# Attention and two expert layers in one kernel: recomputed key blocks, shared PSUM banks, and a move of weight preparation

## The chip, the cores and the metric

The kernel runs on 1 core of a Trainium2 chip. The metric is the device time of the whole program in microseconds (us), as the median of several runs. The profile is one execution recorded by the hardware profiler.

## The reference

Three layers follow each other. N = 8 x 3072 = 24576 tokens, D = 256, 8 experts, hidden width F = 1024.

```python
# attention, 8 batches, S = 3072, z has 64 columns
scores = z @ z.T / S                    # the same z on both sides
x = u * (np.maximum(scores, 0) ** 2 @ v)
# first expert layer: all 8 experts on all tokens
P = exp(x @ w_gate - max)               # then 8 rounds of row and column normalisation
y = sum_e P[:, e] * (np.maximum(x @ w1[e], 0) @ w2[e])
# second expert layer: one expert per token (argmax of a cosine), scaled by its gate
out = gate * (np.maximum(y @ w1b[e], 0) @ w2b[e])
```

## The kernel before

All matrices are split into two float16 halves (high and low), and a product is the sum of high x high, high x low and low x high, so a logical product costs three matmuls. The three layers run one after the other on TensorE (PE).

**Attention (the first 2265 us).** There are 8 batches; in each, 6 chunks `qc` of 512 queries, and in each chunk 24 key blocks `kt` of 128 keys: 1152 steps. The scores are symmetric. A *direct* block computes its scores (`emit_S`, two matmuls of 512 columns), ScalarE (ACT) applies ReLU and squares to `hl`, an engine squares once more in float32 (`sq`), and VectorE (DVE) forms the low half (`emit_low`). In chunk `qc` the direct blocks are those with `kt // 4 >= qc`. Blocks with `kt // 4 > qc` are also stored to DRAM (`store`, 256 KB each), and a later chunk, whose *old* blocks `kt // 4 < qc` are the mirror of these, reads them back with a DMA transpose, two key blocks at a time (`load_turned`, 512 KB, into five buffers named `turned` and `ext`). `chunk_order` spreads the old blocks evenly among the 24 steps. `emit_AV` multiplies a block with `v16`: for each of four query tiles one matmul of 512 columns and one of 256 into its own PSUM bank `o0` to `o3`. Scores run 5 steps ahead of `emit_AV` (`LEAD`).

At a chunk's end the four banks are copied to `osb` (two by ACT, two by DVE), and `chunk_end` lets GpSimd (POOL) add the two halves and multiply by `u`. It then makes a float16 split, transposes it by DMA and stores it for the next layer.

**Background.** Side work is cut into generators that `Background` advances by one piece per step: lane `end` (chunk ends), `prep` (the next batch's z and v), `w` (expert weights) and `x` (tiles for the next layer). A lane with rate r moves once in r steps. Lane `w` loads each expert's weights twice (maximum, then split), writes the split weights to DRAM, first for the first expert layer (m = 0, rate 1.0) and then for the second (m = 1, rate 1.45), and must be done before the last chunk but one. The SP queue issues all these DMAs in the order in which the program is written, and each transfer is cut into packets that 16 DMA engines move.

**First expert layer (about 2265 to 9790 us).** 768 units, each a quarter of an expert on 1024 tokens: 21 matmuls of 512 columns (line 856) and 48 of 256 columns (line 938), with sums on DVE, ACT and POOL. `tick` moves the lanes four times per unit. The 12 superblocks have 64 units each. `tile_end` finishes each 512 tokens: it picks the expert, and writes a row with the token's split values, its expert's scale `iab` and gate.

**Second expert layer (from about 9790 us).** 67 jobs of 512 or 256 tokens of one expert, `job_first` (line 1377) and `job_second` (lines 924, 925), then `evac2`, which scales the result by a number from the row.

Of the kernel before, what the change touches and what calls it, by code (L numbers as in the profile page):

```python
# [4 lines left out]
F32 = mybir.dt.float32  # L5
# [6 lines left out]
P = 128  # L12
D = 256
# [73 lines left out]
def program(tc, u, v, z, wg, w1a, w2a, emb, tau, w1b, w2b, out, pool, psum, dram):  # L87
# [14 lines left out]
    wd = [dram.tile([E, P, W1N + 8 * 512], F16, name="wd0"), dram.tile([E, P, 2, 8 * 512], F16, name="wd1")]  # L102
    rows_d = dram.tile([E * R + PART, ROW], F16, name="rows_d")

    def small(name, n=1, dt=F32):
# [31 lines left out]
    def all_max(dst, src, n, waits=4):  # L137

        d = dram.tile([P, n], F32, name="amax_d")
        SP.dma_start(out=d, in_=src)  # L140
        for _ in range(waits):
            yield
        rows = small(("junk0", "prod5")[n - 1], n * P)
# [73 lines left out]
    raw = []  # L217
    loads = []

    def next_raw():  # L220

        while loads and len(raw) < 3:
            raw.append(loads.pop(0)())
        return raw.pop(0)
# [9 lines left out]
    def weight_scales(m, e):  # L234
# [25 lines left out]
        )  # L260
        yield

    def pair_split(t, e, c, o, s):
# [236 lines left out]

    def chunk_end(b, qc, osb, ut):
        T0 = (b * QC + qc) * 4
        w = m4([P, 4, D], F32, "w")
        for t in range(4):
            o = osb[t // 2][:, t % 2]
            POOL.tensor_tensor(out=w[:, t, :], in0=o[:, 0:D], in1=o[:, D:2 * D], op=ALU.add)
            yield
        for t in range(4):
            POOL.tensor_tensor(out=w[:, t, :], in0=w[:, t, :], in1=ut[:, t, :], op=ALU.mult)
            yield  # L510
# [57 lines left out]
    bg.lane("prep", 2)  # L568
    bg.lane("w", 1.0)
    bg.lane("x")  # L570
# [69 lines left out]
    with tc.manual_schedule():  # L640
# [8 lines left out]
        for _ in gg:  # L649
            pass  # L650
        def slower():
            bg.lane_rate("w", 1.45)
            return
            yield

        for m in range(2):
            if m:
                bg.add("w", slower())
            for e in range(E):
                plan_loads(m, e)  # L660
                bg.add("w", weight_scales(m, e))
                bg.add("w", weight_split(m, e))

        def chunk_order(qc):
            own, old = list(range(4 * qc, KT)), list(range(4 * qc))
            early = [(2 * j + 3) * len(old) // (2 * KT) > (2 * j + 1) * len(old) // (2 * KT) for j in range(KT)]

            j = LEAD - 1  # L670
            if early[j]:
                k = early.index(False, j)
                early[j], early[k] = False, True
            res = [(old if e else own).pop(0) for e in early]
            assert sorted(res) == list(range(KT))
            return res
# [3 lines left out]
        for b, qc, kt in steps:  # L680
            if kt // 4 >= qc:
# [37 lines left out]
        def emit_S(b, qc, kt):  # L719
# [33 lines left out]
        def store():  # L753
            hl, b, qc, kt = stores.pop(0)
            k = kt % 4 * P
            SP.dma_start(out=stored[b % 2, qc, kt // 4][k:k + P], in_=hl)

        def emit_AV(b, qc, kt, first, last):
            if kt // 4 >= qc:
# [12 lines left out]

        gens = {}

        def attn_pre(i):
            b, qc, kt = steps[i]
            if i % KT == 0 and qc == 0 and b > 0:
                bg.finish("prep", gens[b])
            direct = kt // 4 >= qc
            if direct:  # L780
                emit_S(b, qc, kt)
            if stores:
                store()
            if len(late) > direct:
                emit_low()

        def attn_main(i):
# [33 lines left out]
def moe(tc, st):  # L821
# [220 lines left out]
    def tile_end(i, x2):  # L1042
# [86 lines left out]
        yield  # L1129
        DVE.tensor_tensor(out=key, in0=oh, in1=iab[1][:, None, :].to_broadcast([P, 4, E]), op=ALU.mult)  # L1130
        DVE.tensor_reduce(out=km, in_=key, op=ALU.add, axis=AX.X)
        yield
        row32 = row.rearrange("p t c -> p (t c)").bitcast(F32).rearrange("p (t c) -> p t c", t=4)
        DVE.scalar_tensor_tensor(out=km, in0=ab, scalar=0.25, in1=km, op0=ALU.mult, op1=ALU.mult)
        DVE.tensor_tensor(out=row32[:, :, 256], in0=km, in1=gt, op=ALU.mult)
        yield
# [182 lines left out]
    def load_job_weights(j):  # L1319
# [8 lines left out]
        SP.dma_start(out=w2t, in_=src[bass.ds(re, 1), :, 1, :].rearrange("o p (f d) -> p (o f) d", f=8))  # L1328
        tab["w", j] = (w1t, w2t)

# [11 lines left out]
    def evac2(j):  # L1342
        ids = tab.pop(("x", j))[1]
        nt = job_size(j) // P
        y = m4([P, nt, D], F32, "yo")
        for t in range(nt):
            c = ids[:, t, 0:1].bitcast(F32)
            s = pool.tile([P, TOK], F32, name="r", tag="r", bufs=3)
# [160 lines left out]
```

## Time and profile before

| what | value |
|---|---|
| median of 3 runs | 10973.49 us (10967.61 to 10974.76) |
| the profiled execution, its own time | 10976.46 us |
| its span | 10974.8 us |
| PE busy over the span | 10573.4 us (96%) |
| DVE, ACT, POOL busy | 6904.8, 4380.1, 3981.6 us |

The shares of the whole span mix three layers with different limits, so each layer has to be read by itself. The DMA share is the mean busy share of the 16 DMA engines. [...]

### The profile page before, as it was taken

What the parts mean: (1) busy time and instruction counts of PE and PEld (TensorE: products, weight loads), DVE (VectorE), ACT (ScalarE), POOL (GpSimd) and SP (SyncE); (2) the same over time, 40 slices, a digit from 0 to 9 for tenths busy, and PEclk for the clock granted to TensorE, in tenths of its full rate; (3) what the DMA queues carried; (4) which work ended last, traced back from release to release, by engine and by line L of the source; (5) the groups of instructions that cost most, each with busy time, mean ns of one, the idle gap of its engine ahead of it and who ended that gap; (6) DMA issues with size and microseconds to landing.
All of it is one profiled execution on the core that took longest, in us unless ns stands there. A gap on an engine that the chain in (4) does not pass through costs nothing. (4 is left out here: it accounts for less than half of the span.)

```text
span 10974.8 us, 181329 instructions
## 1 busy us (share of the span) xinstructions
PE 10573.4 (96%) x72192; PEld 6934.6 (63%) x72192; DVE 6904.8 (63%) x11785; ACT 4380.1 (40%) x7819; POOL 3981.6 (36%) x3649
## 2 busy tenths in 40 slices
PE   7888888899999999999999999999999999999999
PEld 3444444466666666666666666666666666665456
DVE  6777766667666666666665666666666666654333
ACT  4444444433443434444443444444443444333233
POOL 4555555633232233323223333323223332223333
PEclk9999999999999999999999999999999999999999
DMA  7999999831111111111111111111111111125556
GB/s 199 235 235 235 234 236 230 223 91 40 49 50 46 47 46 47 52 42 57 40 55 41 53 42 52 47 42 57 45 48 46 50 49 46 46 80 161 152 168 194
DMA packets 1214292, 1071.97 MB, mean 98 GB/s; under 512 B 931008, under 2 KB 1048256, under 8 KB 1183872
## 3 DMA queue, kind: packets, MB, share of 16 engines
q1 hardware_dynamic: 1194336, 1007.77, 33.4%
q0 software_dynamic: 19104, 52.59, 1.4%
q8 instruction: 565, 9.26, 0.4%
q14 instruction: 287, 2.35, 0.1%
HBM read 592.28 MB, written 245.82 MB: 76 GB/s over the span
## 5 line engine op out<-in xcount | busy, mean ns | idle before, releaser
L938 PE MATMUL o<-w2t,hl 128*128 128x256 f16 x36864 | 4279.2, 273 | 0.0
L938 PEld LDWEIGHTS <-hl 128*128 128x128 f16 x36864 | 3609.2, 98 | 747.5 <-issue 1.1
L856 PE MATMUL r<-xs,w1t 128*128 128x512 f16 x16128 | 3753.8, 379 | 21.5 <-DVE blocks L912 10.9
L911 POOL TENSOR_TENSOR blocks<-prod,terms 128x512 f32<-128x512 f32 x768 | 1339.9, 1745 | 4942.5 <-ACT hl L903 4925.4
L856 PEld LDWEIGHTS <-w1t 128*128 128x128 f16 x16128 | 1568.1, 98 | 1583.5 <-issue 31.4
L892 DVE SCALAR_TENSOR_TENSOR hl<-r,hl 128x512 f16<-128x512 f32 x768 | 531.1, 692 | 1375.3 <-ACT hl L899 1373.9
L899 ACT ACTIVATE hl<-r 128x512 f16<-128x512 f32 x768 | 458.6, 597 | 2055.1 <-PE r L856 2055.1
L892 DVE SCALAR_TENSOR_TENSOR hl<-blocks,hl 128x1024 f16<-128x1024 f32 x768 | 960.5, 1251 | 305.3 <-ACT hl L917 273.2
L885 DVE TENSOR_TENSOR terms<-r,terms 128x512 f32<-128x512 f32 x768 | 530.3, 690 | 817.5 <-ACT prod L881 658.2
L879 ACT ACTIVATE terms<-r 128x512 f32<-128x512 f32 x768 | 458.5, 597 | 1239.6 <-PE r L856 849.8
L903 ACT ACTIVATE hl<-terms 128x512 f16<-128x512 f32 x768 | 484.1, 630 | 1058.6 <-DVE terms L902 1058.6
L917 ACT ACTIVATE hl<-blocks 128x1024 f16<-128x1024 f32 x768 | 807.1, 1051 | 0.0
L770 PE MATMUL o<-v,hl 128*128 128x512 f16 x1792 | 640.1, 393 | 84.3 <-ACT osb L801 50.4
L730 ACT ACTIVATE r<-h 128x512 f32<-128x512 f32 x672 | 397.5, 592 | 798.9 <-PE h L725 739.7
L1383 DVE SCALAR_TENSOR_TENSOR hl<-h,hl 128x512 f16<-128x512 f32 (+1 forms) x536 | 304.1, 568 | 654.2 <-ACT hl L1382 632.9
L1377 PE MATMUL h<-xt,w1t 128*128 128x512 f16 (+1 forms) x3216 | 628.2, 332 | 6.6 <-DVE hl L1383 3.2
L735 POOL TENSOR_TENSOR zt<-r 128x512 f32<-128x512 f32 x336 | 387.3, 1154 | 681.4 <-ACT r L730 625.5
L924 PE MATMUL o<-w2t,hl 128*128 128x512 f16 x1648 | 569.7, 381 | 21.8 <-DVE r L1350 21.0
L770 PE MATMUL o<-v,turned 128*128 128x512 f16 x1536 | 534.0, 389 | 56.0 <-DMA turned<-at 39.6
L892 DVE SCALAR_TENSOR_TENSOR hl<-terms,hl 128x512 f16<-128x512 f32 x768 | 531.9, 693 | 75.9
L1382 ACT ACTIVATE hl<-h 128x512 f16<-128x512 f32 (+1 forms) x536 | 267.3, 499 | 772.6 <-PE h L1377 750.5
L771 PE MATMUL o<-v,hl 128*128 128x256 f16 x1792 | 504.4, 282 | 61.3 <-DVE hl L745 61.1
(240 smaller groups left out, 12613.3 us busy)
## 6 DMA issues: line engine op xcount, KB each, us to landing
w1t<-wd SPq DMA_DIRECT2D x192, 896.0 KB
w2t<-wd SPq DMA_DIRECT2D x163, 1024.0 KB
at<-hl SPq DMA_DIRECT2D x288, 256.0 KB
w1t<-wd SPq DMA_DIRECT2D x67, 1024.0 KB
wraw<-in_moe_w SPq DMA_DIRECT2D x112, 512.0 KB
at<-ext SPq DMA_DIRECT2D x192, 256.0 KB
ut<-in_u SPq DMA_DIRECT2D x48, 512.0 KB
xT_d<-xt SPq DMA_DIRECT2D x48, 512.0 KB
```

Of the source, the lines that this page charges most:

```text
L770: PE.matmul(o, lhsT=tiles[t][0], rhs=vt, start=first, stop=False)
L771: PE.matmul(o[:, D:2 * D], lhsT=tiles[t][1], rhs=vt[:, 0:D], start=False, stop=last)
L856: PE.matmul(r, lhsT=w[:, p % 2, blk, a, :], rhs=x[:, b, :], start=start and j == 0, stop=j == 2, skip_group_check=True,)
L885: DVE.tensor_tensor(out=u2, in0=r[1], in1=c1, op=ALU.add)
L892: eng.scalar_tensor_tensor(out=dst, in0=src, scalar=0.0, in1=hi, op0=ALU.max, op1=ALU.subtract)
L899: ACT.activation(out=f0[:, 0, h0], in_=r[0], func=AF.Relu)
L903: ACT.activation(out=f0[:, 0, h1], in_=c12, func=AF.Relu)
L911: POOL.tensor_tensor(out=terms[1][:, 1], in0=terms[2], in1=u3, op=ALU.add)
L917: ACT.activation(out=f1[:, 0], in_=c2, func=AF.Relu)
L924: PE.matmul(o_ps[t], lhsT=hl[:, 0, t * P:(t + 1) * P], rhs=w2t[:, f, :], start=f == 0, stop=False)
L938: PE.matmul(o, lhsT=hl[:, a, t * P:(t + 1) * P], rhs=w2t[:, f, b * D:(b + 1) * D], start=f == 0 and t % 2 == 0 and a + b == 0, stop=f == 7 ...
L1377: PE.matmul(h, lhsT=w1t[:, a, c, f * P:(f + 1) * P], rhs=xt[:, 2 * b + c, :], start=i == 0, stop=i == 5)
```

## The change

Six edits, all visible in the diff:

1. `direct(qc, kt)` is now `kt // 2 >= 2 * qc - 1`: each chunk from the second on computes two key blocks more itself and reads one pair of blocks less. The half of a stored block that nobody reads any more is not stored.
2. `emit_AV` uses three matmuls of 256 columns for a query tile, and two query tiles share a PSUM bank. Two banks make a set, and chunks alternate between two sets. The copies to `osb` and POOL's additions are gone; `chunk_end` multiplies by `u` straight from PSUM on DVE.
3. The odd extra squares are all on ACT; before, every second of them was on DVE.
4. Lane `w` runs at rate 1.9 through attention and prepares only m = 0. The weights with m = 1 are planned at the start of the second superblock of the first expert layer, at rate 6, with two raw buffers instead of three.
5. Because these weights come later, `tile_end` no longer multiplies by `iab`. It is written to DRAM (`iab_d`), each job loads it (`iabj`), and `evac2` multiplies it in with a small DVE operation.
6. The broadcast row of the weights' maximum uses a buffer of the common pool `m4`.

```diff
-    bg.lane("w", 1.0)
+    bg.lane("w", 1.9)
...
+        def direct(qc, kt):
+            return kt // 2 >= 2 * qc - 1
 
         def chunk_order(qc):
-            own, old = list(range(4 * qc, KT)), list(range(4 * qc))
+            own, old = ([kt for kt in range(KT) if direct(qc, kt) == d] for d in (True, False))
...
             if n % 2 == 0:
                 POOL.tensor_tensor(out=a, in0=r, in1=r, op=ALU.mult)
-            elif n % 4 == 1:
+            else:
                 ACT.activation(out=a, in_=r, func=AF.Square)
-            else:
-                DVE.tensor_tensor(out=a, in0=r, in1=r, op=ALU.mult)
...
-            SP.dma_start(out=stored[b % 2, qc, kt // 4][k:k + P], in_=hl)
+            n = 1 if kt // 4 == qc + 1 else 2
+            SP.dma_start(out=stored[b % 2, qc, kt // 4][k:k + P, 0:n], in_=hl[:, 0:n])
...
-                if first:
-                    acc_ps[t] = psum.tile([P, 2 * D], F32, name=f"o{t}", tag=f"o{t}", bufs=1)
-                o = acc_ps[t]
-                PE.matmul(o, lhsT=tiles[t][0], rhs=vt, start=first, stop=False)
-                PE.matmul(o[:, D:2 * D], lhsT=tiles[t][1], rhs=vt[:, 0:D], start=False, stop=last)
+                if first and t % 2 == 0:
+                    n = (b * QC + qc) % 2 * 2 + t // 2
+                    acc_ps[t // 2] = psum.tile([P, 2 * D], F32, name=f"o{n}", tag=f"o{n}", bufs=1)
+                o = acc_ps[t // 2][:, t % 2 * D:(t % 2 + 1) * D]
+                for a, h in ((0, 0), (0, 1), (1, 0)):
+                    PE.matmul(
+                        o, lhsT=tiles[t][a], rhs=vt[:, h * D:(h + 1) * D], start=first and t % 2 == 0 and a + h == 0,
+                        stop=last and a == 1, skip_group_check=True,
+                    )
...
-                osb = [m4([P, 2, 2 * D], F32, "osb") for _ in range(2)]
-                for t in range(4):
-                    if t % 2:
-                        DVE.tensor_copy(out=osb[t // 2][:, t % 2], in_=acc_ps[t])
-                    else:
-                        ACT.activation(out=osb[t // 2][:, t % 2], in_=acc_ps[t], func=AF.Copy)
                 bg.finish("end")
-                bg.add("end", chunk_end(b, qc, osb, ut.pop((b, qc))))
+                bg.add("end", chunk_end(b, qc, dict(acc_ps), ut.pop((b, qc))))
...
-        for t in range(4):
-            o = osb[t // 2][:, t % 2]
-            POOL.tensor_tensor(out=w[:, t, :], in0=o[:, 0:D], in1=o[:, D:2 * D], op=ALU.add)
-            yield
-        for t in range(4):
-            POOL.tensor_tensor(out=w[:, t, :], in0=w[:, t, :], in1=ut[:, t, :], op=ALU.mult)
+        yield
+        for j in range(2):
+            DVE.tensor_tensor(
+                out=w[:, 2 * j:2 * j + 2, :], in0=acc[j].rearrange("p (t d) -> p t d", t=2),
+                in1=ut[:, 2 * j:2 * j + 2, :], op=ALU.mult,
+            )
             yield
...
+        if (i, e, p) == (SB, 0, 0):
+            g["depth"][0] = 2
+            bg.lane_rate("w", 6)
+            g["plan_weights"](1)
         if i >= NTILE - SB and e == E - 1 and p % 2:
+            bg.finish("w")
...
+        cs = tmp("wb", 4)[:, 0:nt]
+        DVE.tensor_scalar(out=cs, in0=ids[:, :, 0].bitcast(F32), scalar1=tab["w", j][2], scalar2=None, op0=ALU.mult)
```

The first place is the SP queue in the first batch, third chunk (`qc` = 2). Rows with `at` on the left store a block for a later chunk (`at_2_3`: from chunk 2 for chunk 3), `turned` and `ext` are pairs read back, `vring` and `zr` the next batch's v, `wraw` and `wpair` weights, `xt` a chunk end. Before:

```order
L756 DMA at_2_3_226<-hl_67 128x1024
L708 DMA_TRANSPOSE turned<-at_0_3_219 128x4x512
L756 DMA at_2_3_226<-hl_67 128x1024
L285 DMA wd_64<-wpair 128x1792
L756 DMA at_2_3_226<-hl_68 128x1024
L207 DMA wraw<-in_moe_w 128x4x256
L756 DMA at_2_3_226<-hl_68 128x1024
```

And in the changed kernel:

```order
L758 DMA at_2_3_227<-ext 128x512 x2
L758 DMA at_2_3_227<-hl_68 128x512
L392 DMA zt<-zt 64x1024 x4
L407 DMA vring<-in_v 128x2x256 x4
L543 DMA_TRANSPOSE xt<-xr 128x4x128 x4
L758 DMA at_2_3_227<-hl_68 128x512
```

The four stores for the next chunk have half their width, and the weights' DMAs stand further apart.

The second place is DVE at a chunk's end in a middle batch, where `o` is an accumulator bank, `hl` and `ext` are low halves of blocks, and `wraw` is weight work. Before:

```order
L271 TENSOR_TENSOR wraw<-wraw 128x128
L799 COPY osb<-o_4466 128x512
L799 COPY osb<-o_4472 128x512
L494 SCALAR_TENSOR_TENSOR v_4702<-zr,fk,v_4702 128x256 x2
L745 TENSOR_TENSOR hl_67<-zt,hl_67 128x2x256
```

And in the changed kernel:

```order
L746 TENSOR_TENSOR hl_69<-zt,hl_69 128x2x256
L510 TENSOR_TENSOR w<-o_7171,ut 128x512
L271 TENSOR_TENSOR wraw<-wraw 128x128
L272 TENSOR_TENSOR wraw<-wraw 128x128
L746 TENSOR_TENSOR ext<-zt,ext 128x2x256
L510 TENSOR_TENSOR w<-o_7178,ut 128x512
```

The two copies that stood together at the chunk's end became two products, one step apart and behind low halves of the next chunk.

The third place is DVE in the first expert layer, in one and the same unit (`terms`, `blocks` and `hl` are the unit's own sums, `acc` an expert's end). Before:

```order
L912 TENSOR_TENSOR blocks<-r_33133,terms 128x512
L1220 SCALAR_TENSOR_TENSOR acc<-o_32884,L,acc 128x256 x2
L1220 SCALAR_TENSOR_TENSOR acc<-o_32898,L,acc 128x256 x2
L885 TENSOR_TENSOR terms<-r_33223,terms 128x512
L892 SCALAR_TENSOR_TENSOR hl_21440<-blocks,hl_21440 128x1024
```

And in the changed kernel:

```order
L915 TENSOR_TENSOR blocks<-r_37038,terms 128x512
L1219 SCALAR_TENSOR_TENSOR acc<-o_36783,L,acc 128x256 x2
L1219 SCALAR_TENSOR_TENSOR acc<-o_36797,L,acc 128x256 x2
L319 SCALAR_TENSOR_TENSOR wout<-wraw,sc_79,wout 128x256
L888 TENSOR_TENSOR terms<-r_37128,terms 128x512
L895 SCALAR_TENSOR_TENSOR hl_25298<-blocks,hl_25298 128x1024
```

One weight operation stands ahead of the unit's own sums.

## Rows read from the trace of the kernel before

**Rows 1.** The page's span in 40 equal slices: DMA share in tenths.

```profile
DMA  7999999831111111111111111111111111125556
```

**Rows 2.** Busy time by stretch: attention, batches 3 and 8, and inner stretches.

```profile
core 0: us, PE busy (x) PEld busy (x) DVE busy (x) ACT busy (x) POOL busy (x), PEclk, DMA share, GB/s
41.00:2265.00 2224.00, 1925.70 (x11313) 1071.09 (x11312) 1533.73 (x2734) 958.21 (x1689) 1252.86 (x1405) 0.95 0.93 230
...
625.00:907.00 282.00, 241.55 (x1417) 133.30 (x1416) 202.78 (x376) 118.91 (x207) 156.60 (x176) 0.96 0.95 239
...
2008.00:2265.00 257.00, 237.36 (x1418) 133.85 (x1417) 158.82 (x255) 123.30 (x232) 159.53 (x174) 0.95 0.83 225
...
500.00:2000.00 1500.00, 1297.87 (x7630) 721.73 (x7631) 1036.84 (x1871) 620.06 (x1083) 848.61 (x960) 0.95 0.97 233
3000.00:9000.00 6000.00, 5995.89 (x43180) 4145.25 (x43179) 3885.85 (x6433) 2449.26 (x4351) 1863.88 (x1416) 1.00 0.15 48
```

**Rows 3.** DMA view from 500 to 2000 us: packets by size, and two kinds of issues.

```profile
DMA packets 611371, 349.50 MB, mean 233 GB/s; under 512 B 470379, under 2 KB 550325, under 8 KB 611253
...
turned<-at SPq DMA_TRANSPOSE x136
...
ext<-at SPq DMA_TRANSPOSE x34
```

**Rows 4.** DMA view from 3000 to 9000 us.

```profile
DMA packets 130469, 289.56 MB, mean 48 GB/s; under 512 B 90576, under 2 KB 90576, under 8 KB 120144
```

**Rows 5.** Groups by line, 41 to 2265 us: busy us, mean ns, idle before and releasers.

```profile
L770 PE MATMUL o<-v,hl 128*128 128x512 f16 x1792 | 640.1, 393 | 84.3 <-ACT osb L801 50.4 <-DVE osb L799 25.9 <-ACT hl L732 7.9
L770 PE MATMUL o<-v,turned 128*128 128x512 f16 x1536 | 534.0, 389 | 56.0 <-DMA turned<-at 39.6 <-DVE osb L799 15.5 <-ACT osb L801 0.6
...
L735 POOL TENSOR_TENSOR zt<-r 128x512 f32<-128x512 f32 x335 | 386.0, 1154 | 681.2 <-ACT r L730 625.3 <-DVE hl L745 28.7 <-DVE ext L745 10.9
L745 DVE TENSOR_TENSOR hl<-zt,hl 128x512 f16<-128x512 f32 x448 | 378.9, 852 | 200.6 <-POOL zt L735 104.5 <-ACT zt L737 53.6 <-ACT hl L732 40.7
...
L732 ACT ACTIVATE hl<-r 128x512 f16<-128x512 f32 x445 | 280.2, 630 | 208.2 <-DMA at<-hl 188.9 <-DVE hl L745 3.3 <-DVE zb L354 3.3
...
L509 POOL TENSOR_TENSOR w<-w,ut 128x256 f32<-128x256 f32 x188 | 160.5, 870 | 0.0
...
L312 POOL TENSOR_SCALAR wout<-wraw,sc 128x256 f16<-128x256 f32 x192 | 156.2, 819 | 26.4 <-DVE sc L132 14.4 <-DMA zr<-in_v 8.9 <-issue 2.8
...
L243 DVE TENSOR_REDUCE wmx<-wraw 128x1 f32<-128x256 f32 x256 | 101.3, 408 | 40.6 <-DMA wraw<-in_moe_w 40.6
```

**Rows 6.** Timeline from 5000 us: start, duration, engine, instructions.

```profile
5001.67 2.78 PE L938 MATMUL o<-w2t,hl 128*128 128x256 f16 x24
5002.27 1.23 DVE L892 SCALAR_TENSOR_TENSOR hl<-blocks,hl 128x1024 f16<-128x1024 f32 x1 [0.28 <-ACT hl L917]
5004.29 2.10 PE L856 MATMUL r<-xs,w1t 128*128 128x512 f16 x9
...
5006.23 2.78 PE L938 MATMUL o<-w2t,hl 128*128 128x256 f16 x24
```

**Rows 7.** Timeline from 10441 us, the end of a job.

```profile
10442.38 1.26 ACT L1352 ACTIVATE r<-o,ids 128x512 f32<-128x512 f32 x2
...
10442.51 0.69 DVE L1383 SCALAR_TENSOR_TENSOR hl<-h,hl 128x512 f16<-128x512 f32 x1 [1.90 <-ACT hl L1382]
...
10443.12 1.53 DVE L1350 TENSOR_SCALAR r<-o,ids 128x512 f32<-128x512 f32 x2
...
10444.28 0.38 PE L924 MATMUL o<-w2t,hl 128*128 128x512 f16 x1
```

**Rows 8.** Groups by line, 9800 to 10975 us.

```profile
L924 PE MATMUL o<-w2t,hl 128*128 128x512 f16 x1648 | 569.7, 381 | 21.8 <-DVE r L1350 21.0 <-DVE acc L1220 0.6
...
L1063 DVE SCALAR_TENSOR_TENSOR row<-acc,xci,row 128x256 f16<-128x256 f32 x16 | 8.8, 554 | 0.0
```

**Rows 9.** Groups by line, 2800 to 9790 us.

```profile
L1063 DVE SCALAR_TENSOR_TENSOR row<-acc,xci,row 128x256 f16<-128x256 f32 x176 | 143.7, 836 | 0.0
```

More of the change, by code (lines that the diff above doesn't have):

```diff
@@ L103, in program @@
     rows_d = dram.tile([E * R + PART, ROW], F16, name="rows_d")
+    iab_d = dram.tile([E, P], F32, name="iab_d")
     def small(name, n=1, dt=F32):
@@ L142, in all_max @@
             yield
-        rows = small(("junk0", "prod5")[n - 1], n * P)
+        rows = small("junk0", P) if n == 1 else m4([P, n * P], F32, "rows")
         SP.dma_start(out=rows, in_=d.rearrange("p n -> (p n)").partition_broadcast(P))
@@ L218, in program @@
     loads = []
+    depth = [3]
     def next_raw():
-        while loads and len(raw) < 3:
+        while loads and len(raw) < depth[0]:
             raw.append(loads.pop(0)())
@@ L261, in weight_scales @@
         yield
+        if m:
+            SP.dma_start(out=iab_d[e:e + 1, :].rearrange("o p -> p o"), in_=iab[m][:, e:e + 1])
     def pair_split(t, e, c, o, s):
@@ L499, in prep, with chunk_end @@
                     load_pair(KT // 2 + k // 2 + 6)
-    def chunk_end(b, qc, osb, ut):
+    def chunk_end(b, qc, acc, ut):
         T0 = (b * QC + qc) * 4
         w = m4([P, 4, D], F32, "w")
-        for t in range(4):
-            o = osb[t // 2][:, t % 2]
-            POOL.tensor_tensor(out=w[:, t, :], in0=o[:, 0:D], in1=o[:, D:2 * D], op=ALU.add)
-            yield
-        for t in range(4):
-            POOL.tensor_tensor(out=w[:, t, :], in0=w[:, t, :], in1=ut[:, t, :], op=ALU.mult)
+        yield
[4 more added lines that the diff above has]
+            )
             yield
@@ L650, in program, with plan_weights @@
             pass
[L651 to L658, printed above, removed]
+        def plan_weights(m):
             for e in range(E):
@@ L662, in program @@
                 bg.add("w", weight_split(m, e))
+        plan_weights(0)
+        def direct(qc, kt):
+            return kt // 2 >= 2 * qc - 1
         def chunk_order(qc):
-            own, old = list(range(4 * qc, KT)), list(range(4 * qc))
+            own, old = ([kt for kt in range(KT) if direct(qc, kt) == d] for d in (True, False))
             early = [(2 * j + 3) * len(old) // (2 * KT) > (2 * j + 1) * len(old) // (2 * KT) for j in range(KT)]
@@ L680, in program @@
         for b, qc, kt in steps:
-            if kt // 4 >= qc:
+            if direct(qc, kt):
                 number[b, qc, kt] = len(number)
@@ L755, in store @@
             k = kt % 4 * P
-            SP.dma_start(out=stored[b % 2, qc, kt // 4][k:k + P], in_=hl)
+            n = 1 if kt // 4 == qc + 1 else 2
+            SP.dma_start(out=stored[b % 2, qc, kt // 4][k:k + P, 0:n], in_=hl[:, 0:n])
         def emit_AV(b, qc, kt, first, last):
-            if kt // 4 >= qc:
+            if direct(qc, kt):
                 hl = am.pop((b, qc, kt))
@@ L778, in attn_pre @@
                 bg.finish("prep", gens[b])
-            direct = kt // 4 >= qc
-            if direct:
+            new = direct(qc, kt)
+            if new:
                 emit_S(b, qc, kt)
@@ L783, in attn_pre @@
                 store()
-            if len(late) > direct:
+            if len(late) > new:
                 emit_low()
@@ L795, in attn_main @@
             if n == KT - 1:
-                osb = [m4([P, 2, 2 * D], F32, "osb") for _ in range(2)]
-                for t in range(4):
-                    if t % 2:
-                        DVE.tensor_copy(out=osb[t // 2][:, t % 2], in_=acc_ps[t])
-                    else:
-                        ACT.activation(out=osb[t // 2][:, t % 2], in_=acc_ps[t], func=AF.Copy)
                 bg.finish("end")
-                bg.add("end", chunk_end(b, qc, osb, ut.pop((b, qc))))
+                bg.add("end", chunk_end(b, qc, dict(acc_ps), ut.pop((b, qc))))
+                if i == len(steps) - 1:
+                    for _ in range(3):
+                        bg.tick_lane("end")
             if i == len(steps) - 1 - LEAD:
@@ L1129, in tile_end @@
         yield
-        DVE.tensor_tensor(out=key, in0=oh, in1=iab[1][:, None, :].to_broadcast([P, 4, E]), op=ALU.mult)
-        DVE.tensor_reduce(out=km, in_=key, op=ALU.add, axis=AX.X)
-        yield
         row32 = row.rearrange("p t c -> p (t c)").bitcast(F32).rearrange("p (t c) -> p t c", t=4)
-        DVE.scalar_tensor_tensor(out=km, in0=ab, scalar=0.25, in1=km, op0=ALU.mult, op1=ALU.mult)
-        DVE.tensor_tensor(out=row32[:, :, 256], in0=km, in1=gt, op=ALU.mult)
+        DVE.scalar_tensor_tensor(out=row32[:, :, 256], in0=ab, scalar=0.25, in1=gt, op0=ALU.mult, op1=ALU.mult)
         yield
@@ L1328, in load_job_weights @@
         SP.dma_start(out=w2t, in_=src[bass.ds(re, 1), :, 1, :].rearrange("o p (f d) -> p (o f) d", f=8))
-        tab["w", j] = (w1t, w2t)
+        ij = tmp("iabj", 1, bufs=6)
+        SP.dma_start(out=ij, in_=g["iab_d"][bass.ds(re, 1), :].rearrange("o p -> p o"))
+        tab["w", j] = (w1t, w2t, ij)
     def load_job_rows(j):
@@ L1344, in evac2 @@
         nt = job_size(j) // P
+        cs = tmp("wb", 4)[:, 0:nt]
+        DVE.tensor_scalar(out=cs, in0=ids[:, :, 0].bitcast(F32), scalar1=tab["w", j][2], scalar2=None, op0=ALU.mult)
         y = m4([P, nt, D], F32, "yo")
         for t in range(nt):
-            c = ids[:, t, 0:1].bitcast(F32)
+            c = cs[:, t:t + 1]
             s = pool.tile([P, TOK], F32, name="r", tag="r", bufs=3)
```

## The prediction

> **What bounds the kernel now.** The page's slices come first: the DMA engines are nearly full for the first fifth of the span and lightly loaded after it [rows 1]. So the layers have different bounds. The table by stretch shows which [rows 2]. [...] In attention PE works 1925.70 of 2224 us at a mean granted clock of 0.95, while the DMA engines are at 0.93, and at 0.97 between 500 and 2000 us. A batch takes 277.5 us there (1665 us from 343 to 2008 us over six), and its DMA work is some 267 us. DMA is the bound, with PE close behind. The groups of attention fit this [rows 5]: ACT waits 188.9 us before its square for a store to leave the buffer, the low halves on DVE are then late, PE waits 39.6 us for `turned` and another 50.4 + 25.9 + 15.5 + 0.6 = 92 us for the copies to `osb`.
>
> **The price of a DMA.** Two stretches with different mixes give two prices, one per MB and one per packet. From 500 to 2000 us 16 engines worked 0.97 x 1500 x 16 = 23280 us for 349.5 MB in 611371 packets [rows 2, 3]; from 3000 to 9000 us 0.15 x 6000 x 16 = 14400 us for 289.56 MB in 130469 packets [rows 2, 4]. Solved: 43.9 us per MB and 0.013 us per packet, in engine time; over 16 engines that is the time by which the stage gets shorter if DMA alone decides. A transpose moves 256 B a packet: 170 pair loads [rows 3] at 2048 packets are 348 thousand of the 470 thousand packets under 512 B, and `xt`, `zn` and z's rows give most of the rest. A pair then costs (0.524 MB x 43.9 + 2048 x 0.013) / 16 = 3.10 us, a store of 256 KB in 128 packets 0.82 us, half a store 0.46 us.
>
> [...]
>
> **What leaves attention, in DMA time.**
> - m = 1 weights: 64 loads and 32 writes of 512 KB, 50.3 MB, in 26624 packets (rows of 4 KB for w1, 1 KB for w2; writes of 2 and 4 KB): 160 us.
> - 40 pair loads (5 a batch): 124 us.
> - 160 stores halved (20 a batch): 21 MB, same packets, 58 us.
>
> Together 342 us of about 2070 (0.93 x 2224), or 43 a batch.
>
> **What comes to PE.** A product with v is 768 columns for a tile before and after. 24 matmuls of 256 columns take 5004.29 - 5001.67 = 2.62 us with a weight load for each, 0.109 us apiece, and nine of 512 columns 1.94 us, 0.216 apiece [rows 6]. So a step's 12 matmuls cost 1.31 us; the old 4 x (0.216 + 0.109) is 1.30. I cost the split at 4608 x 0.002 = 10 us over the stage, inside the numbers below. 80 more direct blocks cost 2 x 0.216 = 0.43 us each: 34 us.
>
> **Chunk by chunk.** PE at full clock: 24 x 1.31 = 31.4 us plus 0.43 for each direct block. Before, with 24, 20, 16, 12, 8 and 4 of them: 41.7, 40.0, 38.3, 36.6, 34.8, 33.1. DMA: stores 20, 16, 12, 8, 4, 0 and pairs 0, 2, 4, 6, 8, 10 make 142 us of the batch's 267; I spread the other 125 evenly (20.9 a chunk). Then 37.3, 40.2, 43.1, 46.1, 49.0, 51.9. The longer of the two in each chunk sums to 272; measured is 277.5, 2% more. After, with 24, 22, 18, 14, 10, 6 direct blocks PE has 41.7, 40.9, 39.2, 37.4, 35.7, 34.0 (229 in all), and DMA 32.6, 32.4, 35.3, 38.2, 41.1, 45.5 (225; the even part falls by 160 / 48 = 3.3). The longer ones sum to 246.6; with the same 2%, 252 us.
>
> A second way: batch 8 has no next batch to prepare, DMA at 0.83 and 257 us [rows 2]. Without the bank copies' waits (92 / 8 = 11.5 us) and with 4 us more PE work, 250. I take 250 for 277.5: 2224 x 0.099 = 220 us less.
>
> **What the other engines say to it.** DVE loses the squares and 16 + 16 weight operations an expert, and the two products a chunk take the copies' place; POOL loses 384 operations of about 0.87 us [rows 5]. ACT gets 208 squares more and loses 96 copies; in the first chunk of a batch it has two and a half operations a step of about the 0.63 us of line 732 [rows 5], 38 of PE's 41.7 us. That is close, but five steps of lead cover it; its price is nothing, and up to 2 us a batch if the cover fails.
>
> **First expert layer.** It takes on 8 x 16 low halves, 8 x 16 maxima and 8 x 16 POOL operations, one turn of the lane in 1.5 units (some 14.6 us, 376 turns), and 160 us of DMA time at a share of 0.15. DVE works 3885.85 of 6000 us there [rows 2]. The tightest chain that I see has slack: the low half of `blocks` ends at 5003.50 and is used at 5006.23, 2.7 us later [rows 6], where an inserted operation takes 0.41 to 0.84 us. On SP the moved loads wait for a free `m4` buffer, which `tile_end`'s `row` can hold, and the next expert's weights queue behind them; these are issued one expert (8 units, some 78 us) ahead, which covers it. The first two loads have no such lead, so DVE waits for one transfer once. I take +5 us, with bounds 0 and 264 (below).
>
> **Second expert layer.** 67 jobs have one tiny DVE operation between the low half (ending 10443.20) and DVE's evacuation, and ACT's evacuation now waits for it: from 10442.38 to about 10443.4. PE wants the first bank at 10444.28, and ACT's first of two would end near 10444.05 [rows 7]. So long jobs hide it by 0.2 us; in the short ones, where PE already waits 21.0 us for DVE's evacuation [rows 8], some 0.25 us show. The 67 loads of `iabj` go out four jobs ahead with the weights and cost nothing; one that comes late would hold the same evacuation. +8 us, bounds 0 and 67 x 0.6 = 40.
>
> **Sum.** 10976.5 - 220 + 5 + 8 = 10769.5 us for the profiled execution, which is 3 us over the median: 10767 us.
>
> **Rivals.**
> 1. *PE's floor is reached.* If transfers spread well over the chunks, a batch takes PE's 229 us plus 2% for its lower clock, 234: 2224 x 0.157 = 349 less, 10637. For it: DMA is then 225 of 234. Against: that would keep both over 96% busy.
> 2. *Latency stays.* Batch 8 takes 32 us more than PE's 224.5 though DMA is at 0.83. If the waits for the banks only move to other waits, all batches take 257 + 4 = 261: 2224 x 0.059 = 132 less, 10855. For it: the first chunk of a batch is short of neither by the sums above, and ACT's 188.9 us before the square come from a store's latency.
> 3. *The first expert layer pays (slower).* If every moved operation delays PE by its length, 128 x (0.836 + 0.41 + 0.82) = 264 us come back: 10976.5 - 220 + 264 + 8 - 3 = 11025. It turns the sign once each of the 376 turns costs PE more than 0.56 us. The row for line 1063 shows what speaks for it: the same DVE operation takes 836 ns among POOL's work and 554 in the quieter stage [rows 8, 9]. [...]
> 4. *No change*: gain and new costs cancel, 10973.
>
> **How the numbers follow.** About 0.2% (22 us) is what a measurement can tell from no change. The forecast, 245 to 258 us a batch and 10705 to 10830, has 0.62; rival 1 and what lies between, below 10705, 0.15; rival 2, up to 10950, 0.17; no change 0.02; slower 0.04. So faster 0.94, same 0.02, slower 0.04. The range leaves out about one in ten at each end: 10685 to 10865.
>
> **What would show it.** Right: batches of about 250 us with the DMA share near 0.90 and PE's waits for `osb` gone; pair loads 200 instead of 240; PE still over 99.8% busy from 3000 to 9000 us with the weights' rows there; PE's wait for the evacuation in the last layer up by about 8 us. Wrong: batches near 261 with DMA under 0.87 (latency), near 234 with PE over 97% (floor), or PE idle after DVE's `blocks` or `hl` in the first expert layer.

## The result and the profile after

| | before | after |
|---|---|---|
| median of 4 runs each | 10973.83 us | 10728.33 us (10724.91 to 10732.15) |
| ratio, 95% interval | | 0.9778 [0.9761, 0.9794] |
| span of the profiled execution | 10974.8 us | 10726.9 us |
| attention, to the first layer's first product | 2259.9 us | 1995.2 us |
| first expert layer, to the end of its last line 859 product (856 before) | 7576.0 us | 7590.0 us |
| from there to the end | 1138.9 us | 1141.7 us |

The change makes the kernel 2.2% faster, 245 us; 10767 was predicted, with a range of 10685 to 10865. The last three lines are read from the start and end times of PE's products in the profiled execution: attention gives 264.7 us, the first expert layer takes back 14.0, the last layer 2.8.

A line of the page after, the DMA share in 40 slices:

```profile
DMA  8989898411112111211211112121121111125556
```

Beside [rows 1] the DMA engines are no longer full in every slice of attention, and attention ends a slice earlier. The table by stretch after, for attention, for batches 2 to 7, and inside the first expert layer (PEclk is the granted clock as a part of full clock, 1.00):

```profile
44.00:2001.00 1957.00, 1884.90 (x16084) 1525.90 (x16083) 1248.63 (x2335) 1098.73 (x1961) 848.88 (x941) 0.99 0.89 214
303.00:1764.00 1461.00, 1414.83 (x12077) 1145.54 (x12076) 954.08 (x1809) 817.76 (x1447) 641.09 (x706) 0.99 0.92 219
3000.00:9000.00 6000.00, 5979.73 (x42966) 4128.52 (x42965) 4018.68 (x6541) 2430.05 (x4325) 1928.97 (x1535) 1.00 0.18 55
```

The same view of before, for its batches 2 to 7:

```profile
343.00:2008.00 1665.00, 1442.23 (x8497) 801.32 (x8496) 1166.35 (x2094) 711.04 (x1243) 942.86 (x1059) 0.95 0.96 234
```

A sixth of each middle row is one batch: 277.5 us before, 243.5 after. PE was idle 37.1 us of it and is idle 7.7; its busy time falls from 240.4 to 235.8 though it has ten blocks more to compute, because the granted clock went from 0.95 to 0.99. The DMA engines' work falls from 266 us (0.96 x 277.5) to 224 (0.92 x 243.5). In the first expert layer PE, the bound there, was idle 4 us of 6000 [rows 2] and is idle 20, so it is busy 99.7% there and not over the 99.8% that the prediction named.

PE's waits in attention after: us in total, times, longest.

```profile
PE o L774 <- DVE hl L746: 23.3, 14, 12.6
PE o L774 <- DMA turned<-at: 17.8, 8, 5.0
PE pg L557 <- DMA xt<-xr: 13.9, 16, 2.7
```

The 92 us for `osb` [rows 5] are gone, and so is more than half of the wait for `turned` (39.6 to 17.8). One single wait of 12.6 us for a low half, in the first batch, is over half of the largest group; most of the rest is for transfers. Two groups of attention after:

```profile
L746 DVE TENSOR_TENSOR hl<-zt,hl 128x512 f16<-128x512 f32 x502 | 371.7, 746 | 395.0 <-POOL zt L738 160.7 <-ACT zt L740 158.6 <-ACT hl L735 47.8
L735 ACT ACTIVATE hl<-r 128x512 f16<-128x512 f32 x499 | 314.5, 630 | 118.8 <-DMA at<-hl 105.1
```

ACT's wait for a store to leave the buffer falls from 188.9 to 105.1 us, and one low half takes 746 ns where it took 852 [rows 5].

### The profile page after: what moved, and what is told of

Its sections match the earlier page's. It is cut to its first block, busy times and chain, and to the rows that moved or that the text cites. A ratio compares the mean times of both kernels' runs of the same rounds, so it can differ in the third digit from the quotient of the medians.

```text
span 10726.9 us, 190821 instructions
## 1 busy us (share of the span) xinstructions
PE 10530.5 (98%) x76960; PEld 7385.3 (69%) x76960; DVE 6795.4 (63%) x11620; ACT 4507.0 (42%) x8091; POOL 3645.9 (34%) x3305
## 5 line engine op out<-in xcount | busy, mean ns | idle before, releaser
L941 PEld LDWEIGHTS <-hl 128*128 128x128 f16 x36864 | 3608.5, 98 | 749.1 <-DVE hl L895 1.9
L859 PEld LDWEIGHTS <-w1t 128*128 128x128 f16 x16128 | 1567.7, 98 | 1592.9 <-issue 41.1
L774 PE MATMUL o<-v,hl 128*128 128x256 f16 x6024 | 744.0, 275 | 25.2 <-DVE hl L746 23.3
L738 POOL TENSOR_TENSOR zt<-r 128x512 f32<-128x512 f32 x376 | 423.4, 1126 | 994.9 <-ACT r L733 927.6
L774 PEld LDWEIGHTS <-hl 128*128 128x128 f16 x6024 | 591.8, 99 | 186.3 <-DVE hl L746 27.6
L733 ACT ACTIVATE r<-h 128x512 f32<-128x512 f32 x752 | 444.7, 591 | 587.7 <-PE h L728 521.0
L746 DVE TENSOR_TENSOR hl<-zt,hl 128x512 f16<-128x512 f32 x502 | 371.7, 746 | 395.0 <-POOL zt L738 160.7
```

Of the source, the lines that this page charges most:

```text
L774: PE.matmul(o, lhsT=tiles[t][a], rhs=vt[:, h * D:(h + 1) * D], start=first and t % 2 == 0 and a + h == 0, stop=last and a == 1, skip_group ...
L859: PE.matmul(r, lhsT=w[:, p % 2, blk, a, :], rhs=x[:, b, :], start=start and j == 0, stop=j == 2, skip_group_check=True,)
L941: PE.matmul(o, lhsT=hl[:, a, t * P:(t + 1) * P], rhs=w2t[:, f, b * D:(b + 1) * D], start=f == 0 and t % 2 == 0 and a + b == 0, stop=f == 7 ...
```

## The experiments

All were timed beside the kernel before; the ratio is to it. "Batch" is a sixth of the stretch of batches 2 to 7, "DMA" the share of that stretch times the batch. Two limits go with the table. The kernel before had medians from 10966 to 10974 us in these sessions, so a difference between two versions of different sessions is good to some 8 us; the changed kernel (10728.33) was timed in one session only. And the DMA column is no pure measure of work: the bank sets alone move the same 65 MB a batch as the kernel before and read 276 instead of 266.

| kernel | median us | ratio [95%] | batch us | DMA us |
|---|---|---|---|---|
| before | 10966 to 10974 | 1 | 277.5 | 266 |
| weights moved alone | 10860.32 | 0.9904 [0.9888, 0.9921] | 259.2 | 244 |
| recomputed blocks alone | 10900.64 | 0.9941 [0.9925, 0.9958] | 267.8 | 241 |
| bank sets alone | 10950.75 | 0.9982 [0.9972, 0.9992] | 275.7 | 276 |
| after, more DMA work | 10888.48 | 0.9929 [0.9913, 0.9946] | 266.5 | 253 |
| after without bank sets | 10782.61 | 0.9835 [0.9818, 0.9851] | 250.3 | 220 |
| after without recomputed blocks | 10780.25 | 0.9829 [0.9812, 0.9845] | 251.3 | 249 |
| after with DVE's squares | 10758.18 | 0.9809 [0.9793, 0.9825] | 247.7 | 223 |
| after with four old blocks | 10695.62 | 0.9754 [0.9738, 0.9770] | 238.2 | 193 |
| after with moved side work | 10686.98 | 0.9740 [0.9727, 0.9754] | as after | as after |
| both of these | 10658.58 | 0.9714 [0.9700, 0.9727] | | |

Theory A is the prediction's: the DMA engines bound attention, PE is next. Theory B, the rival, is that the engines' waits on each other (for banks and low halves) decide.

**1. The weights alone** (before with edits 4 to 6: edits 1 to 3 taken back).

```diff
-            return kt // 2 >= 2 * qc - 1
+            return kt // 4 >= qc
...
-                    n = (b * QC + qc) % 2 * 2 + t // 2
-                    acc_ps[t // 2] = psum.tile([P, 2 * D], F32, name=f"o{n}", tag=f"o{n}", bufs=1)
+                    acc_ps[t] = psum.tile([P, 2 * D], F32, name=f"o{t}", tag=f"o{t}", bufs=1)
```

> The kernel before with one part of the change: the second layer's weights are prepared in the first expert layer (edits 4 to 6), nothing else. Theory A (the DMA engines bound attention, PE is next): 160 us of DMA time leave attention, 20 us a batch; the longer of the two per chunk sums to 259 us instead of 272, so about 18 us a batch and 150 us in all less in attention, and some 13 to 17 us more in the two expert layers: 10840 us, DMA share still over 0.93. Rival B (the engines' waits for PSUM banks, squares and POOL decide, and the DMA queue is only full because it runs ahead): PE's waits for the banks stay at about 92 us and the gain is under 50 us: over 10925 us.

109 us less, between the two theories and nearer to A (some 130). In the profiled execution attention is 146 us shorter, as A says, and the first expert layer takes back 22. Batches 2 to 7, and waits of PE in attention:

```profile
313.00:1868.00 1555.00, 1416.50 (x8502) 796.57 (x8501) 1087.83 (x1877) 713.93 (x1245) 885.14 (x964) 0.97 0.94 226
```
```profile
PE o L774 <- ACT osb L805: 47.8, 12, 7.9
PE o L774 <- DMA turned<-at: 39.2, 24, 5.3
PE o L774 <- DVE osb L803: 12.0, 13, 2.2
```

DMA work fell by 22 us a batch, the batch by 18. The waits for the banks fell from 92 us to 60, and the weights also took work from DVE (1087.83 us, 1166.35 before) and from POOL (885.14, 942.86 before). This run alone therefore does not tell DMA time from DVE time; experiment 4 does.

**2. The recomputed blocks alone** (before with edit 1).

```diff
-            if kt // 4 >= qc:
+            if direct(qc, kt):
...
+            n = 1 if kt // 4 == qc + 1 else 2
```

> The kernel before with two more key blocks a chunk computed directly (edit 1), nothing else. Theory A: 182 us of DMA time leave and 34 us of PE work come; by the sum of the longer one per chunk 257 us a batch instead of 272, about 165 us less in all: 10810 us. Rival B: PE, ACT, DVE and POOL all get more work and the waits at the banks stay, so nothing or a loss: 10950 to 11020 us.

Neither came true: 69 us less. The stretch and PE's waits:

```profile
332.00:1939.00 1607.00, 1453.52 (x8616) 808.54 (x8615) 1243.47 (x2169) 784.98 (x1378) 998.69 (x1089) 0.96 0.90 222
```
```profile
PE o L775 <- DVE hl L748: 63.2, 54, 14.0
PE o L774 <- DVE osb L803: 52.2, 25, 5.8
PE o L774 <- ACT osb L805: 37.3, 18, 4.5
```

The DMA share fell to 0.90, and PE's wait for `turned` from 39.6 us [rows 5] to 1.8, and still the batch takes 267.8 us: the waits for the copies stayed at 90 us (92 before), and DVE has more to do than before (1243.47 us, 1166.35 before). A holds only until these waits decide. The low halves are no later than before: the first of these waits was 61.1 us there.

**3. The bank sets alone** (before with edits 2, 5 and 6; weights prepared when they were).

```diff
-                        DVE.tensor_copy(out=osb[t // 2][:, t % 2], in_=acc_ps[t])
...
-                        ACT.activation(out=osb[t // 2][:, t % 2], in_=acc_ps[t], func=AF.Copy)
...
+                bg.add("end", chunk_end(b, qc, dict(acc_ps), ut.pop((b, qc))))
```

> The kernel before with the accumulators of two tiles in one bank, two sets, and the product with u from PSUM (edit 2; edits 5 and 6 are in it too, which touch only the last layer's scale). Theory A: the DMA work of attention stays at 267 us a batch, so the waits for the banks (92 us in all) only move to other waits: 0 to 30 us less, 10945 to 10985 us, DMA share 0.93 to 0.95. Rival B: the 92 us and POOL's 330 us of freed work come through: 10880 us or less.

As A says: 18.5 us. The copies that made PE wait 92 us are gone, and the time is not:

```profile
341.00:1995.00 1654.00, 1450.20 (x11957) 1146.77 (x11955) 1086.08 (x2094) 665.85 (x1172) 682.69 (x772) 0.95 1.00 235
```
```profile
PE o L783 <- DMA turned<-at: 83.7, 43, 5.3
PE o L783 <- DVE hl L755: 57.4, 41, 13.9
PE o L783 <- DVE ext L755: 54.9, 27, 9.0
```

The DMA share rose to 1.00, and PE waits for `turned` instead (39.6 before [rows 5], 83.7 up to 2110 us here) and somewhat longer for the low halves (`hl` and `ext` together 95 before, 112 here). In the profiled execution attention is 24 us shorter; the first expert layer is 8 us shorter too and the last 7 longer, where edit 5 is in this version as well.

**4. More DMA work and nothing else** (after, with 96 writes of a constant 0.5 MB in packets of 256 B to spare memory, 12 a batch).

```diff
+            if n % 12 == 8:
+                SP.dma_start(
+                    out=spare[i // 12 % 4].rearrange("p (r c) -> p r c", r=16),
+                    in_=ones16[:, None, :].to_broadcast([P, 16, P]),
+                )
```

> The changed kernel with DMA work put back that nobody waits for: two writes a chunk of a constant to a spare place in DRAM, 2048 packets of 256 B each, 96 in all, about 3.1 us of DMA time each, 37 us a batch. Theory A: DMA is again the longer side, 223 + 37 = 260 us a batch at the 0.96 of before, 270 us: about 213 us longer, 10940 us. Rival B: no engine has more to do and nobody waits for the writes: under 60 us longer, below 10790 us.

160 us slower than after, nearer to A's 213 than to B's 60. The DMA work rose by 29 us a batch (2.4 us a write; I had priced them as pairs at 3.1), the batch by 23:

```profile
316.00:1915.00 1599.00, 1462.82 (x12076) 1165.22 (x12075) 951.51 (x1809) 810.62 (x1447) 638.96 (x706) 0.95 0.95 224
```
```profile
PE pg L558 <- DMA xt<-xr: 76.6, 72, 5.0
PE o L775 <- DMA turned<-at: 39.7, 13, 7.9
```

Six batches by 23 are 138; by the start times the first batch adds 17 and the last 7, together 162, about the 160 of the whole. No engine has anything more to compute, PE waits for transfers, its clock falls from 0.99 to 0.95. This shows that DMA time decides at this load.

**5. Without the bank sets** (after without edit 2).

```diff
-                    PE.matmul(
-                        o, lhsT=tiles[t][a], rhs=vt[:, h * D:(h + 1) * D], start=first and t % 2 == 0 and a + h == 0,
-                        stop=last and a == 1, skip_group_check=True,
-                    )
...
+                PE.matmul(o, lhsT=tiles[t][0], rhs=vt, start=first, stop=False)
+                PE.matmul(o[:, D:2 * D], lhsT=tiles[t][1], rhs=vt[:, 0:D], start=False, stop=last)
```

> The changed kernel without edit 2: four single banks again, copied to osb by ACT and DVE, with POOL's additions and products. Alone, edit 2 gave 18 us. Theory C (a wait at the banks costs nothing while the DMA engines bound attention, and its full length once they don't): PE waits some 90 us for the copies again as it did with the keys alone, and POOL and DVE delay low halves: 70 to 100 us more than the changed kernel, 10800 to 10830 us. Rival D (the edits add up): 18 to 25 us more, about 10750 us.

54 us slower than after, between the two theories: "additive" says 18.5, C 70 to 100. With the DMA share at 0.88 the waits for the copies are back on PE's path, though at 45 us and not at the 90 of C:

```profile
307.00:1809.00 1502.00, 1415.96 (x8619) 804.71 (x8617) 1057.80 (x1810) 853.54 (x1519) 888.90 (x994) 0.98 0.88 213
```
```profile
PE o L773 <- DVE hl L746: 30.5, 19, 13.4
PE o L772 <- ACT osb L803: 30.5, 17, 3.5
PE o L772 <- DVE osb L801: 14.4, 15, 2.8
```

**6. DVE's squares back** (after without edit 3).

```diff
-            else:
+            elif n % 4 == 1:
                 ACT.activation(out=a, in_=r, func=AF.Square)
+            else:
+                DVE.tensor_tensor(out=a, in0=r, in1=r, op=ALU.mult)
```

> The changed kernel without edit 3: every second odd square is on DVE again, some 190 of 0.87 us. By my forecast (price nothing: ACT has room, DVE too): 0 to 15 us more, 10730 to 10745 us. Rival: ACT's 0.9 of the first chunk in a batch was the closer limit, so 5 us a batch less: 10690 us.

30 us slower than after, twice the 15 that I expected at most. The squares were not free on DVE: PE waits oftener for the low half (26 times; 14 after) and for the scores' banks (11 times; 3 after).

```profile
PE o L776 <- DVE hl L748: 30.2, 26, 12.6
PE h L728 <- ACT r L733: 15.9, 11, 3.5
```

**7. Without the recomputed blocks** (after without edit 1).

```diff
-            return kt // 2 >= 2 * qc - 1
+            return kt // 4 >= qc
...
-            n = 1 if kt // 4 == qc + 1 else 2
+            n = 2
```

> The changed kernel without edit 1: old key blocks are read back as before, so 182 us of DMA time return and 34 us of PE work go. Theory C: DMA is the bound again at 244 us a batch with some 0.96 of it busy, 253 us: 75 to 85 us more, about 10808 us. Rival (PE is now the bound and the recomputed blocks only add to it): 0 to 34 us less, 10695 to 10730 us.

52 us slower than after (C said 75 to 85, the rival a gain), and the DMA engines are full again:

```profile
312.00:1820.00 1508.00, 1405.63 (x11955) 1137.49 (x11954) 922.64 (x1749) 734.13 (x1297) 591.75 (x676) 0.98 0.99 233
```
```profile
PE o L774 <- DMA turned<-at: 60.7, 33, 6.0
```

**8. Four old blocks** (after, with four old key blocks of each chunk recomputed instead of two, and no store of a block that only the next chunk would read).

```diff
-            return kt // 2 >= 2 * qc - 1
+            return kt // 2 >= 2 * qc - 2
...
-            if kt // 4 > qc:
+            if kt // 4 > qc + 1:
...
-            n = 1 if kt // 4 == qc + 1 else 2
+            n = 2
```

> The changed kernel with four old key blocks a chunk recomputed instead of two, and blocks of the next chunk's keys not stored at all. By the chunk sum DMA falls from 225 to 200 us a batch, PE rises by 4.3 to 233 (with the logits' small matmuls some 238). If what is left over PE's floor in the changed kernel (243 us a batch against 234) is DMA: the excess goes and PE's work comes, 239 to 243 us a batch, 10695 to 10730 us. If it is other waits: 247 us a batch, 10760 us.

33 us faster than after. PE has ten more blocks a batch to compute, 4.3 us, and the batch is 5.3 us shorter, so what the changed kernel had left over PE's work was DMA, the first of the two readings:

```profile
297.00:1726.00 1429.00, 1419.45 (x12199) 1149.83 (x12198) 1010.25 (x1869) 906.80 (x1597) 680.38 (x736) 1.00 0.81 201
```

PE works 1419 of 1429 us at full clock: here it is the bound.

**9. Side work moved behind the sums** (after; in the first expert layer lane `w` advances after the unit's last sum, not before its sums, and not in units that end an expert; in the last layer `evac2`'s scalar product is made two steps earlier).

```diff
-        bg.tick(count[0], misc=misc)
+        bg.tick(count[0], misc=misc, skip=("w",))
...
+        elif i >= SB:
+            turns[0] += 1
+            if int((turns[0] + 1) / 1.35) > int(turns[0] / 1.35):
+                bg.tick_lane("w")
...
+        if f == 5:
+            cs = tab["c", j] = tmp("wb", 4)[:, 0:n // P]
...
-        cs = tmp("wb", 4)[:, 0:nt]
+        cs = tab.pop(("c", j))
```

> The changed kernel with two costs moved out of the way: in the first expert layer the weights' lane gets its turn behind the unit's last sum instead of ahead of it (not in units that end an expert), and in the last layer the small product with iabj stands two steps ahead of the evacuation. If the first expert layer's longer superblocks (631 instead of 629 us, with the weights among them) come from weight operations ahead of the sum that frees a PSUM bank: superblocks back to 629, 15 to 20 us less; and the last layer's 3 us back: 10708 to 10714 us. If they come from POOL, the DMA engines or DVE's total load: superblocks stay at 631, and 10725 us.

41 us faster than after, more than expected. The first expert layer takes 7574.0 us (7590.0 after, 7576.0 before), and the last one gets 26 us shorter. PE's wait in the last layer, and for `blocks` in the first, here from 2300 to 9500 us, where it is 11.7 us in 19 waits after and 7.1 in 19 before:

```profile
PE o L927 <- DVE r L1352: 12.7, 13, 2.3
```
```profile
PE r L859 <- DVE blocks L915: 4.9, 14, 0.6
```

**10. Both** (8 and 9 together).

> The same two moves together with four recomputed key blocks a chunk. If the three gains lie in three separate layers they add up: 10696 less 15 to 20 us, 10676 to 10682 us.

10658.58 us (10652.7 to 10659.25), 20 us below what I expected, 315 below before and 70 below the changed kernel: the best version of this study.

## Why the prediction was right, and where it was off

**Bound and direction: right.** Attention was bound by the DMA engines, and the change takes 42 us of DMA work from a batch (43 predicted; 224 us left, 225 predicted). Experiment 4 shows it most directly, since it adds DMA work alone: 160 us. Experiments 1, 3 and 7 agree: the weights moved alone gain 109 us (with some of DVE's and POOL's work), freed banks alone 18.5, and without the recomputed blocks the share is back at 0.99. The two-term price carried over: batches 42 us lighter, as summed from 64 loads, 40 pairs and 160 half stores. Experiment 2 tests the price of a pair: edit 1 takes 25 us of DMA work from a batch (266 to 241), where 3.10 us a pair makes 22.7, and the price of two stores of the same bytes, 1.64, would make 15.4.

**Attention, -220: measured -264.7.** The mis-sized step is "with the same 2%", and its twin, the second way from batch 8. The chunk sum gave 246.6 us a batch; measured are 243.5, just under the 245 to 258 of the forecast, and chunk by chunk (start times of the trace, means of batches 2 to 7) 42.2, 41.0, 43.7, 37.8, 38.5, 40.3 where the longer of PE and DMA was 41.7, 40.9, 39.2, 38.2, 41.1, 45.5. So the sum was close without a surcharge. The DMA work is less bunched at the batch's end than I spread it: the packets' times of the six chunks make 33.2, 34.5, 45.1, 36.2, 39.0 and 34.9 us, where I had 32.6 rising to 45.5.

That the sum came within 2% of before was luck. Its chunks took 48.1, 45.9, 49.4, 43.6, 45.7, 44.7 us, where the sum has 41.7, 40.2, 43.1, 46.1, 49.0, 51.9: up to 7 us too little and 7 too much, and only the total fits. In the first of them neither bound decides, since PE is busy 42.1 us and the DMA engines 35.2; PE waits 5.1 us there for ACT's copies to `osb`, and with the bank sets alone that chunk takes 42.7.

The surcharge of before was therefore no constant: it was made of waits and of PE's clock. The trace of before has one behind the other, here in three stretches of 8 us:

```profile
756.00:764.00 8.00, 7.49 (x51) 4.17 (x48) 7.93 (x19) 4.03 (x7) 1.85 (x1) 1.00 0.98 281
764.00:772.00 8.00, 3.89 (x28) 2.24 (x29) 3.01 (x7) 2.65 (x5) 2.17 (x2) 0.98 0.94 237
772.00:780.00 8.00, 6.97 (x26) 3.31 (x26) 5.62 (x12) 1.23 (x2) 2.54 (x3) 0.59 1.07 252
```

PE idles 4.1 us of the second stretch; in the third (a DMA share over 1 belongs to packets that end after the stretch) the granted clock is 0.59, and it does 26 products in 6.97 us. From 773 to 778 us the clock is 0.50, and the two products with v of a query tile start every 0.64 us; from 765.65 to 768.24, at 1.00, every 0.32. As an estimate, a mean clock of 0.95 is 13.9 us lost in a batch of 277.5, 0.99 is 2.4 in 243.5. Where the waits go, about 11 us of clock come with them, and that had no term of its own. The other side of it: PE's work at full clock is not 229 us. With four old blocks it is busy 236.6 us a batch at 1.00; less ten blocks of 0.43 that is 232 for the changed kernel.

**The banks.** "PE's waits for `osb` gone" came true. What the 92 us were worth depends on the DMA engines: 18.5 us while these are full (3), 54 when they are relieved (5). Single gains of 109, 69 and 18.5 sum to 196; with the squares' 30, some 227 of 245. The 18 us left are hardly more than such differences can tell; that each edit removes the wait to which another's gain would have gone is my reading, and no run shows it alone.

**ACT's squares, "its price is nothing": wrong in sign.** The prediction priced what ACT takes on, and what DVE loses it only named. With 188 squares back on DVE (the other 20 of the 208 belong to recomputed blocks) its busy time in batches 2 to 7 is 1062.97 us instead of 954.08, PE waits for low halves twice as often, and 30 us are lost (6).

**First expert layer, +5: measured +14.0.** The first superblock, in which no such weights are prepared, got 5 us shorter (654.8 to 649.7, start times), the others together 19 longer. The failed step is "the tightest chain that I see has slack": the 2.7 us were read off the low half of `blocks`, in a unit without `tile_end`. The chain that pays is another: the sum `blocks` on DVE, which frees the PSUM bank `r` for PE. The timeline after shows one place, in a unit that ends an expert and where `tile_end` has its turn:

```profile
6715.90 1.26 DVE L1102 TENSOR_TENSOR lg<-lg,xmx 128x32 f32<-128x32 f32 x1
...
6717.07 2.48 POOL L1221 TENSOR_TENSOR acc<-acc,r 128x512 f32<-128x512 f32 x2
6717.08 1.30 DVE L1104 SCALAR_TENSOR_TENSOR key<-key,iota 128x32 f32<-128x32 f32 x1
...
6718.31 1.53 DVE L319 SCALAR_TENSOR_TENSOR wout<-wraw,sc,wout 128x256 f16<-128x256 f32 x1
6719.76 0.68 DVE L915 TENSOR_TENSOR blocks<-r,terms 128x512 f32<-128x512 f32 x1
...
6720.49 0.81 PE L859 MATMUL r<-xs,w1t 128*128 128x512 f16 x3 [2.00 <-DVE blocks L915]
```

Two operations of `tile_end` and one of the weights stand in a row ahead of the unit's sum, and beside POOL's work they take 1.26, 1.30 and 1.53 us. Before, the second of them took 0.18 us in all of its 48 places; after, it falls beside POOL's sum of an expert's end in 6 of 48 and takes 1.30 us in each. From 3000 to 9000 us PE waited for `blocks` 9 times before, 2.3 us in all, and 16 times after, 10.3 us. In the whole layer, before and after:

```profile
PE r L856 <- DVE blocks L912: 10.9, 22, 2.9
```
```profile
PE r L859 <- DVE blocks L915: 15.9, 27, 2.0
```

So rival 3 had the place and not the size. Experiment 9 has the size: with the same operations behind the last sum the layer is 16.0 us shorter, not 264, and superblocks 2 to 12, 6921.2 us before and 6940.3 after, take 6924.5, so they then cost some 3 us.

**Last layer, +8: measured +2.8, by two errors.** "Long jobs hide it by 0.2 us" failed. The end of a long job after, and PE's waits in the layer:

```profile
10115.91 0.22 DVE L1347 TENSOR_SCALAR wb<-ids,iabj 128x4 f32<-128x4 f32 x1
...
10116.25 1.26 ACT L1355 ACTIVATE r<-o,wb 128x512 f32<-128x512 f32 x2 [0.98 <-DVE wb L1347]
...
10117.02 1.40 POOL L1356 TENSOR_TENSOR yo<-r 128x256 f32<-128x256 f32 x2 [4.58 <-ACT r L1355]
...
10117.78 0.75 DVE L1353 TENSOR_SCALAR r<-o,wb 128x512 f32<-128x512 f32 x1 [0.75 <-POOL yo L1356]
```
```profile
PE o L927 <- ACT r L1355: 19.0, 30, 2.4
PE o L927 <- DVE r L1353: 15.3, 35, 1.9
```

ACT stood ready and waits 0.98 us for a DVE operation of 0.22 us. In this long job PE's next product still finds the first bank free, as predicted. What the prediction did not follow is the rest of the chain: POOL's sum starts late because ACT's result is late, DVE's second evacuation waits for that sum to free one of the three `r` buffers, and PE then waits for DVE, 0.37 us in most of the 36 long jobs. In the 31 short jobs PE waits for ACT's evacuation itself, 0.56 us in most. Before, PE waited 21.0 us for DVE's evacuation and never for ACT's [rows 8], so the wait is up by 13 us and not by 8.

With the scalar made earlier the layer is 26 us shorter (9): that is the price of edit 5's small product, some 0.4 us for each of 67 jobs. From the start of the 25th job to the end the layer takes 601.8 us before, 618.9 after and 603.4 in experiment 9 (start times). It shows as 2.8 because the 24 jobs ahead got 14.2 us shorter (537.0 to 522.8), for a reason that the prediction did not have. Before, the clock was 0.98 there (1.00 after), and PE had stalls like this one, with DVE waiting for POOL:

```profile
10087.02 0.75 DVE L1350 TENSOR_SCALAR r<-o,ids 128x512 f32<-128x512 f32 x1 [4.35 <-POOL yo L1353]
...
10087.83 0.58 PE L924 MATMUL o<-w2t,hl 128*128 128x512 f16 x1 [3.60 <-DVE r L1350]
```

The other versions point at edit 5, which also shortens `tile_end`: the bank sets alone and the weights alone, both with edit 5, do these 24 jobs 10.3 and 16.2 us faster than before, the recomputed blocks alone, without it, only 3.2. No run has edit 5 by itself, so that is not shown.

**The rivals.** 1 (floor): not reached by this change, since PE idles 7.7 us a batch, but by experiment 8. 2 (latency): its sign is in experiment 2, where the share is 0.90 and the batch 267.8; the changed kernel escapes because banks and squares go with it (5 and 6: 54 and 30 us). 3: above.

**The total.** Attention gave 45 us more than the sum had, the two expert layers together took 4 us more than the sum's 13. So 10728 instead of 10767 is attention's error almost alone.

## What to carry to other kernels

Here 92 us of waits were worth 18.5 us while the DMA engines were full, and 45 us of the same waits cost 54 when they were not: take the DMA work away first, then the waits, and price the two together. Where transfers bound a stage, compute again what is cheap to compute (here 0.43 us of PE for a block against half of a pair load of 3.1 us and half or all of a store of 0.82), until PE runs at full clock almost without waits (1419 of 1429 us at 1.00, experiment 8). Put side work behind the operation that frees a PSUM bank or ends a sum, not ahead of it, even where it is short: 0.22 us of DVE a job cost 26 us here. And test a sum by stages against each stage of the kernel before, not against its total alone.

## What was unexpected of the hardware

- Waits cost twice here: the idle time, and then work at a lower granted clock (0.50 from 773 to 778 us, above). Between before and the version with four old blocks the granted clock in batches 2 to 7 goes 0.95, 0.99, 1.00, while PE idles 37.1, 7.7 and 1.6 us of a batch. With added transfers alone (experiment 4) PE idles 22.7 us of a batch instead of 7.7, and the clock is 0.95 instead of 0.99.
- The time of a DVE operation goes with what POOL does beside it. The same low half takes 852 ns in the kernel before, with POOL busy 1252.86 of 2224 us [rows 2, 5], and 746 with 848.88 of 1957; in batches 2 to 7 (tile `hl`) 848 before and 749 after, and edit 2 takes POOL's additions and products at the chunk's end away. Of the 448 low halves before, 131 meet no POOL operation and 68 start ahead of the one that they meet: none of these takes over 694 ns. The other 249 start while POOL works and take 986 ns in the mean. In the changed kernel line 1102's operation of 128x32 elements takes 1.25 to 1.26 us in the 44 of 48 places where a POOL sum runs as it starts, and ends 0.05 us after that sum; in the other four it takes 0.18. Line 1104's takes 1.30 us in 6 places, again to 0.05 us after POOL's sum, and 0.18 to 0.19 in the other 42; before it took 0.18 in all 48. No run took POOL's work away alone, since edit 2 also takes two copies a chunk from DVE, and no run shows what in the two engines makes it so.
- The price by MB and packet, 3.1 us for 0.5 MB in 2048 packets, was too high for plain writes of that kind: 2.4 us of DMA time each (experiment 4: 29 us for 12).
